# Moving a turn's second output addition, re-timing the steady table and merging the last two stores of a fused attention and feed-forward kernel

## The chip, the cores and the metric

The kernel runs on one core of a Trainium2 chip. The metric is the device time of one execution in microseconds (us). A program of one core is timed several times and the median is given. One more execution is taken with the hardware profiler, and every row below comes from that one.

## What is computed

The inputs are q, k and v of 8 batches, 8 heads, 576 tokens and 64 channels, phi of 32 memories for each token and head, and two weight matrices. The reference, cut to what matters:

```python
a = softmax(phi, axis=memories)
k_m, v_m = einsum("bhsm,bhsd->bhmd", a, k), einsum("bhsm,bhsd->bhmd", a, v)
attn = softmax(q @ k_m.T / sqrt(64)) @ v_m           # 32 memories per head
x = attn.transpose(0, 2, 1, 3).reshape(4608, 512)    # 8 batches of 576 tokens
h = x @ w_in                                         # 512 -> 2048
out = (h * clip(h + 3, 0, 6) / 6) @ w_out            # 2048 -> 512
```

All of it is float32. The kernel keeps that accuracy on TensorE by splitting each operand into a rounded high part and a low remainder, and by multiplying three times (high by high, high by low, low by high).

## The kernel before

v_m is never multiplied with the probabilities by itself. For each batch the kernel first folds v_m into w_in ("fold", line 457, in four chunks of 512 columns, names `fo.b.c`), so that the first product is probabilities times folded weights (`gemm1`, line 746, into the two PSUM tiles `ph`). The gated result goes into a second product with w_out (`products`, through `triple`, line 713). The folded weights come out of PSUM as a high part (`vh`, ScalarE, line 468) and a low part (`vl`, VectorE, line 477).

The first two batches run in an order that is written out word by word (`BEGIN`). The rest, from some 203 us on, is the steady part. A batch there is 32 **steps**; the tables `STEADY` and `EVERY` give each word of the attention work a step (`4 fo.C.3` means: in step 4, fold chunk 3 of the current batch C; N is the next batch, M the one after). A batch has two halves of 256 and 320 tokens, a half has eight **units**, and a unit takes two steps, one for each of its two 128-row pieces of the hidden layer:

- Step 2n: TensorE does `gemm1`, ScalarE `relu` (line 752), VectorE `gate` (line 765); ScalarE and VectorE split the first four blocks of the unit before into high and low (`high`, line 786, `low`, line 791, tiles of 512 columns).
- Step 2n+1: the same for the second piece, then the sums that the product scheme needs: `sum_first` on VectorE (line 775), `sum_second` on GpSimd (lines 779 and 780), and the split of three more blocks (384 columns).
- In both, the products of the unit of three steps before, and in every even step the loads of the w_out blocks ("streams", line 709) of the unit two ahead, three DMAs of 256 KB on SP's queue.

The scheme is one level of a seven-product block multiplication, so a half's result stands in four PSUM banks that have to be combined: this is the **turn**, in steps 1 to 4 and 17 to 20. `leave_first` and `leave_second` read the banks (ScalarE lines 819, 820, 825; VectorE lines 828, 829), `leave_third` does two additions on GpSimd (lines 833 and 834) and `store` writes the tile (line 839). The list `owed` holds what is still to be done: at the next odd step, behind that unit's sums, `leave_third` is called, and at the even step after it `store`.

The last 64 tokens of each batch ("rests") are collected for two batches and multiplied in a stage of their own at step 2 of every even batch and at the end (`rest_stage`). At an even batch the turn's additions and store, and the words of steps 0 to 2, are played inside that stage. At the very end `RestUnit.leave` reads two PSUM tiles of 256 columns with ScalarE (line 889) and stores each as two pieces of 64 rows, one for each batch (line 892): three pieces on SP's queue and the last on ScalarE's.

Loads run on SP's queue in the order of the program; a DMA that has to wait (for a buffer, for example) holds up those behind it. The w_in chunks lie in a ring of two tiles (`fetch.b.c.half`, line 213, 512 KB each), and five further buffers (`KV_RING`) are shared by the k and v tiles (line 234), the q tiles (line 244) and phi (line 228). The k and v tiles of a batch are last read by `mem.N` in step 11 (line 319, 80 matmuls).

Of the kernel before, what the change touches and what calls it, by code (L numbers as in the profile page):

```python
# [19 lines left out]
B, H, S, D, M = 8, 8, 576, 64, 32  # L20
# [6 lines left out]
REST = S - 4 * P  # L27
# [10 lines left out]
VC = 256  # L38
# [53 lines left out]
"""  # L92

STEADY = """
1 fo.C.3 vh.C.3.0 / 4 vl.C.3.0 / 8 vh.C.3.1 / 9 bh.C.1 vl.C.3.1 / 14 bl.C.1
"""

EVERY = """
2 sp.N / 7 xa.N.0 / 8 xe.N.0 xa.N.2 fetch.N.1.0 / 9 xe.N.2 xa.N.1 xe.N.1 / 10 fetch.N.0.0 / 11 mem.N / 12 q.N.1 nr.N
nk.N pt.M fetch.N.0.1 q.N.0 / 15 tp.N fetch.N.1.1 tk.N / 16 sb.N cp.N.2 / 17 cp.N.0 / 19 kv.M.0 cp.N.1 / 20 cm.N.0 /  # L100
21 fo.N.0 cm.N.1 / 22 cs.N.0 / 23 mx.M.0 vh.N.0.0 kv.M.1 vh.N.0.1 fetch.N.2.0 ex.N.0 vl.N.0.0 vl.N.0.1 ds.N.0
fetch.N.2.1 / 24 cs.N.1 mx.M.1 / 25 fo.N.1 vh.N.1.0 vl.N.1.0 dr.N.0 dm.N.0 / 26 fetch.N.3.0 vh.N.1.1 ex.N.1 pn.M
vl.N.1.1 mt.M bt.N.0 / 27 ds.N.1 kv.M.2 / 28 fo.N.2 vh.N.2.0 dr.N.1 dm.N.1 bh.N.0 kv.M.3 vl.N.2.0 / 29 kv.M.4 mo.M
fetch.N.3.1 bl.N.0 / 31 vh.N.2.1 bt.N.1 vl.N.2.1
"""

LATE = ()
# [3 lines left out]
def attention_ffn_kernel(ctx: ExitStack, tc: tile.TileContext, pn, pt, kv, kl, qt, w1, w2, out):  # L111
    nc = tc.nc
# [5 lines left out]
    sb = ctx.enter_context(tc.tile_pool(name="sb", bufs=1))  # L118
# [610 lines left out]
    class Unit:  # L729
# [101 lines left out]
        def leave_third(self):  # L831
            o, x = self.o, self.x
            nc.gpsimd.tensor_tensor(o[:, 1:3], x[:, 0:2], x[:, 2:4], ALU.add)
            nc.gpsimd.tensor_tensor(o[:, 0::3], o[:, 0::3], x[:, 1:3], ALU.add)

        def store(self):
# [7 lines left out]
    class RestUnit:  # L844
# [40 lines left out]
        def leave(self):  # L885
            if self.b == B - 2:
                for c in range(2):
                    o = sb.tile([P, VC], F32, name="o", **O_RING)
                    nc.scalar.mul(o, sums[self.b, 2][c], 1.0 / 6.0)
                    for k, queue in enumerate((nc.sync, nc.scalar if c else nc.sync)):  # L890
                        row = (self.b + k + 1) * S - REST
                        queue.dma_start(
                            out=out[row : row + REST, c * VC : (c + 1) * VC], in_=o[k * REST : (k + 1) * REST]
                        )
                return
            o = sb.tile([P, DM], F32, name="o", **O_RING)
            nc.scalar.mul(o[:, :VC], sums[self.b, 2][0], 1.0 / 6.0)
            nc.vector.tensor_scalar(o[:, VC:], sums[self.b, 2][1], 1.0 / 6.0, None, ALU.mult)
            for k in range(2):
                row = (self.b + k + 1) * S - REST  # L900
                nc.sync.dma_start(out=out[row : row + REST], in_=o[k * REST : (k + 1) * REST])
# [64 lines left out]
    with tc.manual_schedule():  # L966
# [32 lines left out]
        def half_step(i, between=None):  # L999
# [9 lines left out]
            unit, part = units[i // 2], i % 2  # L1009
# [8 lines left out]
            if unit.last:  # L1018
                (unit.leave_second if part else unit.leave_first)()
                if part and not between:  # L1020
                    owed[:] = unit.leave_third, unit.store
            return unit

        def finish_unit(unit, part):
# [13 lines left out]
        owed = []  # L1038
        total_steps = 2 * len(units)
        for s in range(total_steps + LAG + 1):  # L1040
# [8 lines left out]
            if s < total_steps:  # L1049
# [8 lines left out]
                if k:  # L1058
                    unit.sum_first()
                    unit.sum_second()  # L1060
                    if owed and len(owed) == 2:
                        owed.pop(0)()
                elif s >= 2 and not (resting and i == 2):
                    finish_unit(units[s // 2 - 1], 1)
# [8 lines left out]
                us[i].prepare()  # L1073
            unit = half_step(s - LAG - 1, (lambda: (us[3].total(), us[3].prepare())) if resting and i == 2 else None)
            if resting and i == 2:
                after = {2: [unit.leave_third, unit.store]} if unit else {}
                if b < B:
                    first = units[s // 2 - 1]
                    for k in range(3):
# [52 lines left out]
```

## Time and profile before

| | |
|---|---|
| median of 3 runs | 679.83 us (679.71 to 680.68) |
| the profiled execution's own time | 679.15 us |
| its span, first to last instruction | 677.3 us |
| TensorE matmul busy | 664.7 us, 98% of the span |
| VectorE / ScalarE / GpSimd busy | 567.9 / 397.0 / 350.8 us |
| DMA, mean over the span | 242 GB/s |

Matmuls overlap in the pipeline: one of 256 columns is listed with some 280 ns, while the next begins 113 ns after it. So the time between the starts of neighbouring matmuls tells what a matmul costs, and the busy share says little of how full the engine is. "Idle before" in a row is idle time of the engine ahead of it, with what ended it.

### The profile page before, as it was taken

The numbers are of one execution on the slowest core, as the hardware profiler recorded it, in microseconds if no ns is written. First come the engines' busy times: TensorE is split into PE (matmuls) and PEld (weight loads), VectorE is DVE, ScalarE is ACT, GpSimd is POOL, SyncE is SP. The second block draws the span as 40 slices with busy tenths as digits, with TensorE's granted clock in tenths as the row PEclk, the third lists the DMA queues.
The fourth block names the chain that finished last, engine by engine and source line by source line (L and its number), as shares of the span: only waits on it lengthen the run. The fifth ranks groups of instructions, "written<-read, shape, count | busy, mean of one in ns | idle before, by whom it ended". The sixth has DMA issues, their size and how long they took to land.

```text
span 677.3 us, 15517 instructions
## 1 busy us (share of the span) xinstructions
PE 664.7 (98%) x5890; PEld 579.3 (86%) x5894; DVE 567.9 (84%) x1070; ACT 397.0 (59%) x819; POOL 350.8 (52%) x356
## 2 busy tenths in 40 slices
PE   8999999999999999999999999999999999999997
PEld 3446787778779998899899998899989999899997
DVE  4899998988996779887997879977899779887865
ACT  4586787574654556655665655655565555655553
POOL 1644243898573337453654345554556246555533
PEclk9999999999999999999999999999999999999999
DMA  9998492355858968769591786949493594836351
GB/s 352 419 334 314 176 378 95 151 180 170 325 183 280 353 251 278 310 209 363 179 395 48 223 334 184 398 150 360 173 370 146 181 312 127 279 113 230 126 187 47
DMA packets 66820, 163.96 MB, mean 242 GB/s; under 512 B 7097, under 2 KB 12217, under 8 KB 64697
## 3 DMA queue, kind: packets, MB, share of 16 engines
q1 hardware_dynamic: 66664, 162.91, 67.4%
q8 instruction: 46, 0.75, 0.4%
q14 instruction: 30, 0.24, 0.1%
q10 hardware_dynamic: 80, 0.07, 0.0%
HBM read 140.92 MB, written 22.03 MB: 241 GB/s over the span
## 4 chain that ended last, share of the span: by engine, by line
PE 80%; DVE 12%; DMA 3%; ACT 3%; issue 1%; POOL 0%; SPq 0%; ACTq 0%; DVEq 0%
PE acc L713 35%; PE ph L746 18%; PE acc L574 10%; PE ph L520 7%; PE pv L457 4%; DVE rounded L791 3%; PE pk L319 2%; PE acc L911 2%; DMA w<-w_kept 2%; DVE gated L765 1%; DVE gated L775 1%; DVE both L477 1%; PE psc L387 1%; ACT rounded L786 1%; DVE gf L536 1%
## 5 line engine op out<-in xcount | busy, mean ns | idle before, releaser
L713 PE MATMUL acc<-w,rounded 128*128 128x256 f32 x1536 | 212.3, 280 | 1.6 <-DVE rounded L791 1.4
L713 PEld LDWEIGHTS acc<-w,rounded 128*128 128x128 f32 x1536 | 192.1, 188 | 21.9 <-ACT gf L752 11.7
L779 POOL TENSOR_TENSOR gated<-gated 128x256 f32<-128x256 f32 x96 | 92.9, 968 | 216.4 <-DVE gated L765 210.2
L791 DVE TENSOR_TENSOR rounded<-gated,rounded 128x384 fp32r<-128x384 f32 x192 | 158.0, 824 | 36.6 <-ACT rounded L786 35.9
L746 PE MATMUL ph<-probs,both 128*128 128x256 f32 (+1 forms) x1152 | 180.6, 292 | 0.0
L786 ACT CAST rounded<-gated 128x384 fp32r<-128x384 f32 x192 | 108.6, 567 | 112.7 <-DVE gated L775 103.4
L746 PEld LDWEIGHTS ph<-probs,both 128*128 128x128 f32 x1152 | 157.5, 188 | 1.0 <-issue 0.8
L752 ACT ACTIVATE gf<-ph,three 128x256 f32<-128x256 f32 (+1 forms) x192 | 95.9, 499 | 46.5 <-PE ph L746 45.4
L713 PE MATMUL acc<-stream,rounded 128*128 128x256 f32 x864 | 113.7, 276 | 0.0
L713 PEld LDWEIGHTS acc<-stream,rounded 128*128 128x128 f32 x864 | 105.2, 188 | 0.0
L765 DVE SCALAR_TENSOR_TENSOR gated<-gf,ph 128x256 f32<-128x256 f32 x192 | 79.0, 412 | 27.7 <-ACT gf L752 26.8
L574 PE MATMUL acc<-w,ghi 128*128 128x512 f32 x224 | 59.0, 396 | 0.0
L520 PEld LDWEIGHTS ph<-probs,both 128*128 128x128 f32 x336 | 47.1, 188 | 10.4 <-DVE gf L536 5.8
L520 PE MATMUL ph<-probs,both 128*128 128x320 f32 (+1 forms) x336 | 51.1, 299 | 1.4 <-DVE gf L536 0.9
L574 PEld LDWEIGHTS acc<-w,ghi 128*128 128x128 f32 x224 | 40.1, 188 | 10.9 <-ACT gf L530 1.7
L780 POOL TENSOR_TENSOR gated<-gated 128x128 f32<-128x128 f32 x96 | 49.1, 512 | 0.0
L775 DVE TENSOR_TENSOR gated<-gated 128x256 f32<-128x256 f32 x96 | 42.2, 439 | 1.6
L468 ACT CAST both<-pv 128x512 fp32r<-128x512 f32 x62 | 35.5, 585 | 13.5 <-PE pv L457 12.7
L477 DVE TENSOR_TENSOR both<-pv,both 128x512 fp32r<-128x512 f32 x62 | 41.1, 673 | 1.8 <-ACT both L468 1.5
L190 POOL TENSOR_TENSOR w<-tmp,raw 128x512 uint32<-128x512 uint32 x12 | 18.9, 1595 | 44.5 <-DVE tmp L180 27.1
L530 ACT ACTIVATE gf<-ph,three 128x576 f32<-128x576 f32 (+2 forms) x36 | 24.7, 690 | 23.2 <-PE ph L520 13.7
L457 PE MATMUL pv<-w,kvT 64*32 64x512 f32 (+1 forms) x528 | 35.1, 588 | 2.2 <-DMA w<-w_kept 0.9
(124 smaller groups left out, 862.5 us busy)
## 6 DMA issues: line engine op xcount, KB each, us to landing
stream<-kept SPq DMA_DIRECT2D x222, 256.0 KB, 4.5
w<-w_kept SPq DMA_DIRECT2D x40, 512.0 KB, 6.8
kvt<-in_kv SPq DMA_DIRECT2D x32, 516.0 KB, 6.2
raw<-in_w SPq DMA_DIRECT2D x16, 512.0 KB, 9.5
raw<-in_w SPq DMA_DIRECT2D x8, 1024.0 KB, 10.3
out_t<-o SPq DMA_DIRECT2D x16, 512.0 KB, 3.1
kept<-stage SPq DMA_DIRECT2D x24, 256.0 KB, 2.7
pnat<-in_pn SPq DMA_DIRECT2D x8, 576.0 KB, 7.9
```

Source lines behind the costliest of these rows:

```text
L457: nc.tensor.matmul(to[j * M : (j + 1) * M, g, k], self.kvT[rows, g, j * M : (j + 1) * M], chunk[rows, k, j].bitcast(F32), start=True, stop ...
L520: nc.tensor.matmul(dst, w[:, g, fs], x[:, g * n : (g + 1) * n], start=(i == 0), stop=(i == len(seq) - 1),)
L574: nc.tensor.matmul(accs[self.b, self.rest, k].rearrange("p (x c) -> p x c", c=VC), left[:, t * P : (t + 1) * P], w, start=k in self.first ...
L713: nc.tensor.matmul(dst, left[l], right[r], start=begin and n == 0, stop=end and n == 2, skip_group_check=True)
L746: nc.tensor.matmul(h, w[:, g, fs], x[:, g * self.n : (g + 1) * self.n], start=(i == 0), stop=(i == len(seq) - 1))
L752: nc.scalar.activation(self.gf, self.h[k], AF.Relu, bias=three)
L765: nc.vector.scalar_tensor_tensor(dst, by_tile(self.gf), 6.0, by_tile(self.h[k]), ALU.min, ALU.mult)
L775: nc.vector.tensor_tensor(g[:, 5:7], g[:, 7:9], g[:, 0:2], ALU.add)
L779: nc.gpsimd.tensor_tensor(g[:, 2:4], g[:, 0::8], g[:, 1:8:6], ALU.subtract)
L780: nc.gpsimd.tensor_tensor(g[:, 4], g[:, 1], g[:, 7], ALU.add)
L786: nc.scalar.copy(self.parts[0][:, at], self.g[:, 1:8][:, at])
L791: nc.vector.tensor_tensor(low[:, at], self.g[:, 1:8][:, at], high[:, at].bitcast(F32), ALU.subtract)
```

## The change

- `leave_third` is cut in two. Its second addition becomes `leave_fourth`, and `owed` now holds three calls. At a turn outside the rest stage the first addition stays behind the sums of the next odd step, the second comes behind those of the odd step after that, and the store two steps later than before. In the rest stage the order stays as it was.
- The steady tables are written anew. The fourth chunk's fold goes from step 1 to step 4 (with its `vh` and `vl`), one phi subtraction and exponential change places (`xa`, `xe`), q is loaded from step 9 instead of 12, the second half of chunk 0 returns at step 17 instead of 12, the k and v loads come earlier, the scores' transposes (`cp`) all in step 16.
- The last two stores: each tile of 128 rows is now written by one DMA, whose destination is seen as 2 batches by 64 rows by 256 columns; the first on SP's queue, the second on ScalarE's.

```diff
 STEADY = """
-1 fo.C.3 vh.C.3.0 / 4 vl.C.3.0 / 8 vh.C.3.1 / 9 bh.C.1 vl.C.3.1 / 14 bl.C.1
+4 fo.C.3 / 5 vh.C.3.0 vl.C.3.0 / 6 vh.C.3.1 / 8 bh.C.1 vl.C.3.1 / 14 bl.C.1
 """
 EVERY = """
-2 sp.N / 7 xa.N.0 / 8 xe.N.0 xa.N.2 fetch.N.1.0 / 9 xe.N.2 xa.N.1 xe.N.1 / 10 fetch.N.0.0 / 11 mem.N / 12 q.N.1 nr.N
-nk.N pt.M fetch.N.0.1 q.N.0 / 15 tp.N fetch.N.1.1 tk.N / 16 sb.N cp.N.2 / 17 cp.N.0 / 19 kv.M.0 cp.N.1 / 20 cm.N.0 /
...
+4 sp.N / 7 xa.N.0 / 8 fetch.N.0.0 xa.N.1 xe.N.0 fetch.N.1.0 / 9 q.N.1 xe.N.1 q.N.0 xa.N.2 / 10 xe.N.2 / 11 mem.N / 12
+nr.N nk.N / 14 pt.M / 15 tp.N tk.N / 16 cp.N.0 fetch.N.1.1 sb.N kv.M.0 cp.N.1 cp.N.2 / 17 fetch.N.0.1 / 20 cm.N.0 / 21
...
         def leave_third(self):
             o, x = self.o, self.x
             nc.gpsimd.tensor_tensor(o[:, 1:3], x[:, 0:2], x[:, 2:4], ALU.add)
+
+        def leave_fourth(self):
+            o, x = self.o, self.x
             nc.gpsimd.tensor_tensor(o[:, 0::3], o[:, 0::3], x[:, 1:3], ALU.add)
...
-                    for k, queue in enumerate((nc.sync, nc.scalar if c else nc.sync)):
-                        row = (self.b + k + 1) * S - REST
-                        queue.dma_start(
-                            out=out[row : row + REST, c * VC : (c + 1) * VC], in_=o[k * REST : (k + 1) * REST]
-                        )
+                    both = out[self.b * S :].rearrange("(k s) d -> k s d", k=2)[:, S - REST :]
+                    queue = nc.scalar if c else nc.sync
+                    queue.dma_start(
+                        out=both[:, :, c * VC : (c + 1) * VC], in_=o
+                    )
...
-                    owed[:] = unit.leave_third, unit.store
+                    owed[:] = unit.leave_third, unit.leave_fourth, unit.store
...
-                    if owed and len(owed) == 2:
+                    if len(owed) > 1:
                         owed.pop(0)()
...
-                after = {2: [unit.leave_third, unit.store]} if unit else {}
+                after = {2: [unit.leave_third, unit.leave_fourth, unit.store]} if unit else {}
```

**First place: VectorE, steps 3 to 6 of an odd batch, just behind the turn.** `both<-pv` is the low part of a folded chunk (`vl`), the other names are those of the section above. Before:

```order
L791 TENSOR_TENSOR rounded<-gated,rounded 128x512
L477 TENSOR_TENSOR both<-pv,both 128x512
L765 SCALAR_TENSOR_TENSOR gated<-gf,ph_2144 128x256
L775 TENSOR_TENSOR gated<-gated 128x256
L791 TENSOR_TENSOR rounded<-gated,rounded 128x384
```

and now:

```order
L791 TENSOR_TENSOR rounded<-gated,rounded 128x512
L765 SCALAR_TENSOR_TENSOR gated<-gf,ph_2144 128x256
L775 TENSOR_TENSOR gated<-gated 128x256
L477 TENSOR_TENSOR both<-pv,both 128x512
L791 TENSOR_TENSOR rounded<-gated,rounded 128x384
```

The low part of the folded chunk no longer stands ahead of step 5's gate, but behind its sum. On GpSimd the same stretch read before:

```order
L833 TENSOR_TENSOR o<-o 128x512
L834 TENSOR_TENSOR o<-o 128x2x256
L779 TENSOR_TENSOR gated<-gated 128x256
L780 TENSOR_TENSOR gated<-gated 128x128
L779 TENSOR_TENSOR gated<-gated 128x256
```

and now:

```order
L833 TENSOR_TENSOR o<-o 128x512
L779 TENSOR_TENSOR gated<-gated 128x256
L780 TENSOR_TENSOR gated<-gated 128x128
L837 TENSOR_TENSOR o<-o 128x2x256
L779 TENSOR_TENSOR gated<-gated 128x256
```

The second addition (834, now 837) stands behind the sums of step 5 instead of ahead of them.

**Second place: SP's queue, steps 10 to 14.** `kept_1_106` and its like are the three blocks of one unit's stream (here of the unit whose second part runs in step 14), `qh` the q tiles. Before:

```order
L213 DMA w_5029<-w_kept_81 128x1024
L709 DMA stream<-kept_1_106 128x512
L709 DMA stream<-kept_2_107 128x512
L709 DMA stream<-kept_0_105 128x512
L244 DMA qh<-in_qt 128x640 x2
L228 DMA ptile<-in_pt 128x576 x2
L213 DMA w_5029<-w_kept_81 128x1024
L244 DMA qh<-in_qt 128x1024
```

and now:

```order
L244 DMA qh<-in_qt 128x640 x2
L244 DMA qh<-in_qt 128x1024
L709 DMA stream<-kept_1_106 128x512
L709 DMA stream<-kept_2_107 128x512
L709 DMA stream<-kept_0_105 128x512
```

The q loads, whose buffers are those of the k and v tiles that step 11 reads, now stand ahead of step 10's stream.

**Third place: the end of ScalarE's queue.** Before:

```order
L865 CAST rounded<-total 128x128
L889 ACTIVATE o<-acc 128x256 x2
L892 DMA out_t<-o 64x256
L1128 UNCONDITIONAL_BRANCH
```

and now:

```order
L868 CAST rounded<-total 128x128
L892 ACTIVATE o<-acc 128x256 x2
L895 DMA out_t<-o 2x64x256
L1131 UNCONDITIONAL_BRANCH
```

The DMA's size is that of its destination: 64 rows of 256 before, 2 by 64 rows of 256 now. On SP's queue three such stores of 64 rows became one of 2 by 64.

## Rows read from the trace of the kernel before

**Rows 1.** Waits of PE: line waited for, us in total, times, longest.
```profile
PE acc L713 <- DVE rounded L791: 1.4, 4, 0.4
PE pv L457 <- DMA w<-w_kept: 0.9, 2, 0.6
```
**Rows 2.** PE's timeline at the fourth chunk's fold, batches 3 and 5: start us, us, what.
```profile
282.59 0.84 PE L746 MATMUL ph<-probs,both 128*128 128x256 f32 x6
283.69 1.09 PE L457 MATMUL pv<-w,kvT 64*32 64x512 f32 x16 [0.26 <-DMA w<-w_kept]
...
438.46 0.87 PE L746 MATMUL ph<-probs,both 128*128 128x256 f32 x6
439.97 1.09 PE L457 MATMUL pv<-w,kvT 64*32 64x512 f32 x16 [0.65 <-DMA w<-w_kept]
```
**Rows 3.** The same timeline at an undisturbed fold (step 21).
```profile
327.25 1.03 PE L746 MATMUL ph<-probs,both 128*128 128x320 f32 x6
328.22 1.09 PE L457 MATMUL pv<-w,kvT 64*32 64x512 f32 x16
```
**Rows 4.** PE's timeline at step 7 of batch 3, and step 23 of batch 7.
```profile
296.05 0.39 PE L713 MATMUL acc<-w,rounded 128*128 128x256 f32 x2
296.78 1.08 PE L713 MATMUL acc<-w,rounded 128*128 128x256 f32 x7 [0.34 <-DVE rounded L791]
...
639.93 1.56 PE L713 MATMUL acc<-w,rounded 128*128 128x256 f32 x9
```
**Rows 5.** The chain of waits from 290 to 297 us, its end.
```profile
292.48 1.37 DVE rounded L791
293.85 0.60 DVE both L477
...
295.87 0.86 DVE rounded L791
```
**Rows 6.** GpSimd's timeline in the same stretch.
```profile
291.69 1.61 POOL L833 TENSOR_TENSOR o<-o 128x512 f32<-128x512 f32 x1
293.26 1.74 POOL L834 TENSOR_TENSOR o<-o 128x512 f32<-128x512 f32 x1
```
**Rows 7.** VectorE's and PE's timeline at steps 6 to 9 of batch 3.
```profile
296.99 0.69 DVE L791 TENSOR_TENSOR rounded<-gated,rounded 128x512 fp32r<-128x512 f32 x1
...
299.54 0.81 DVE L791 TENSOR_TENSOR rounded<-gated,rounded 128x384 fp32r<-128x384 f32 x1
...
300.41 1.18 PE L713 MATMUL acc<-w,rounded 128*128 128x256 f32 x9
```
**Rows 8.** PE's timeline at steps 11 to 14 of batch 3.
```profile
306.52 1.30 PE L713 MATMUL acc<-w,rounded 128*128 128x256 f32 x9
...
312.43 0.84 PE L713 MATMUL acc<-stream,rounded 128*128 128x256 f32 x6
```
**Rows 9.** DMA issues from 303 to 313 us: KB each, median us to landing.
```profile
stream<-kept SPq DMA_DIRECT2D x7, 256.0 KB, 6.5
```
**Rows 10.** Timeline from 672.5 us: the last DMA issues of SP and ScalarE.
```profile
673.09 1.75 SPq L892 DMA_DIRECT2D out_t<-o  x3
...
673.78 0.56 ACTq L892 DMA_DIRECT2D out_t<-o  x1
```
**Rows 11.** DMA from 670 to 677.3 us: GB/s in 40 slices; packets by queue.
```profile
GB/s 0 0 0 0 0 0 0 0 0 0 0 0 0 0 0 0 0 0 0 0 0 0 0 151 185 23 50 208 219 208 191 185 17 0 0 0 0 0 0 0
...
q10 hardware_dynamic: 80, 0.07, 3.7%
...
out_t<-o ACTq DMA_DIRECT2D x1, 64.0 KB, 2.2
```
**Rows 12.** DMA from 70.8 to 73 us, around the store of the maxima.
```profile
DMA packets 48, 0.28 MB, mean 125 GB/s; under 512 B 13, under 2 KB 13, under 8 KB 16
...
nmx<-nmxT SPq DMA_DIRECT2D x1, 1.0 KB
```
**Rows 13.** DMA from 142.6 to 144.4 us, stores of 1 KB rows: GB/s, 40 slices.
```profile
GB/s 91 205 296 364 341 364 319 364 364 319 296 364 341 319 387 364 341 342 342 364 319 319 364 341 319 364 387 341 364 319 341 341 341 319 524 228 524 159 592 364
```

More of the change, by code (lines that the diff above doesn't have):

```diff
@@ L94 @@
 STEADY = """
-1 fo.C.3 vh.C.3.0 / 4 vl.C.3.0 / 8 vh.C.3.1 / 9 bh.C.1 vl.C.3.1 / 14 bl.C.1
+4 fo.C.3 / 5 vh.C.3.0 vl.C.3.0 / 6 vh.C.3.1 / 8 bh.C.1 vl.C.3.1 / 14 bl.C.1
 """
 EVERY = """
-2 sp.N / 7 xa.N.0 / 8 xe.N.0 xa.N.2 fetch.N.1.0 / 9 xe.N.2 xa.N.1 xe.N.1 / 10 fetch.N.0.0 / 11 mem.N / 12 q.N.1 nr.N
-nk.N pt.M fetch.N.0.1 q.N.0 / 15 tp.N fetch.N.1.1 tk.N / 16 sb.N cp.N.2 / 17 cp.N.0 / 19 kv.M.0 cp.N.1 / 20 cm.N.0 /
[L101 to L104, printed above, removed]
+4 sp.N / 7 xa.N.0 / 8 fetch.N.0.0 xa.N.1 xe.N.0 fetch.N.1.0 / 9 q.N.1 xe.N.1 q.N.0 xa.N.2 / 10 xe.N.2 / 11 mem.N / 12
+nr.N nk.N / 14 pt.M / 15 tp.N tk.N / 16 cp.N.0 fetch.N.1.1 sb.N kv.M.0 cp.N.1 cp.N.2 / 17 fetch.N.0.1 / 20 cm.N.0 / 21
+cm.N.1 fo.N.0 / 22 cs.N.0 kv.M.1 / 23 mx.M.0 vh.N.0.0 kv.M.4 kv.M.2 cs.N.1 vh.N.0.1 fetch.N.2.0 ex.N.0 vl.N.0.0
+vl.N.0.1 ds.N.0 fetch.N.2.1 / 24 mx.M.1 / 25 fo.N.1 vh.N.1.0 vl.N.1.0 fetch.N.3.0 dr.N.0 dm.N.0 / 26 vh.N.1.1 ex.N.1
+vl.N.1.1 mt.M bt.N.0 pn.M / 27 ds.N.1 dr.N.1 mo.M / 28 fo.N.2 fetch.N.3.1 dm.N.1 vh.N.2.0 bh.N.0 kv.M.3 / 29 vl.N.2.0
+/ 30 vh.N.2.1 bl.N.0 / 31 vl.N.2.1 bt.N.1
 """
```

## The prediction

> **What bounds the kernel now.** I read the page first: TensorE is busy for 98% of the span, so only two kinds of time can go: time in which TensorE waits, and what follows its last matmul. The waits of PE say how little the first is: 1.4 us behind VectorE's low part (line 791) in 4 places, 0.9 us behind the return of a w_in chunk in 2 [rows 1]. Everything else that this change moves lies beside matmuls. These waits are counted from a modelled end, so I size them again from starts in PE's timeline; for what leads up to them I read the chain of waits there, GpSimd's timeline beside it, and the DMA view for the loads and the last stores.
>
> **What the fold's move gives.** At an undisturbed fold, six matmuls of 320 columns start at 327.25 and the fold at 328.22, 0.97 later [rows 3]; at 0.147 a matmul that is 0.88 and 0.09 for the switch. Six of 256 columns at 0.113 make 0.68 + 0.09 = 0.77. In batch 3 the fold came 283.69 - 282.59 = 1.10 after its predecessors, 0.33 late; in batch 5 439.97 - 438.46 = 1.51, 0.74 late [rows 2]. Both wait for the second half of chunk 3. In step 4 instead of 1, with that load issued a step earlier, the fold has some four steps or 8 us to spare where it was short of 0.74, so both waits go: **-1.07 us**. The fold's own 1.09 [rows 3] moves whole, and costs the same in step 4 as in step 1.
>
> **What the turn gives.** In step 7 of batch 3 two products start at 296.05; the third should start 0.23 later, at 296.28, and starts at 296.78: 0.50 lost, and 0.11 more, since the seven that follow take 1.08 [rows 4] where 6 x 0.113 + 0.28 = 0.97 is usual. Two more such places, in step 7 of batches 5 and 7, measure the same (the 4 of [rows 1]), and step 23 of batch 7 loses 0.38: nine matmuls take 1.56 [rows 4] where 1.18 is usual [rows 7]. Together 3 x 0.61 + 0.38 = 2.21 us. The chain there runs through VectorE alone: the 512-column low part takes 1.37, then the folded chunk's low part 0.60, then the gate [rows 5]. The 512-column part takes 0.69 elsewhere [rows 7]; here GpSimd's two additions, 1.61 and 1.74 long, run beside it [rows 6]. The change takes both out of the way: the folded chunk's part goes behind the gate and the sum, where VectorE waited for ScalarE anyway, and the second addition goes behind the next sums. Step 4's fold gives VectorE another 1 us ahead of step 5. **-2.21 us.**
>
> **What is late next.** The second addition now runs beside the 512-column low part of step 6, which can take 1.37 for 0.69 there: up to 0.7 later. The low part of step 7 ended at 299.54 + 0.81 = 300.35, and the products that need it began at 300.41 [rows 7]: 0.06 to spare in the old order. From the new order I count about 0.1 of reserve, so some of it will come back. It costs nothing at best and 0.7 at worst, in batches 3 and 5 (batch 7 has no phi work there); I take 0.2 each, since the fold's 1 us stands ahead: **+0.4**. The rest of the tables I cost at nothing. The transposes of step 16 fall into a stretch in which VectorE waited for ScalarE; the later phi remainder must be through ScalarE before the last of the 80 memory matmuls, which I count to be met by 0.1 to 0.5; chunk 0's second half returns in step 17 for a fold in step 21, four steps or 8 us for a load that [rows 9] let take 6 to 7. The store two steps later frees a buffer that is wanted 12 steps on.
>
> **What the last stores cost.** This term decides. Now four stores of 64 rows leave at 673.09 (three on SP, 1.75 together) and 673.78 (ScalarE) [rows 10]; bytes flow from 674.2 (slice 24) to 676.0 (slice 33) [rows 11]. Merging spares SP two issues. But how many DMA engines carry a store follows its shape. A store of 64 rows counts 80 packets, 64 rows and 16 closing ones, one for each engine [rows 11]. The store of the maxima, 4 by 2 pieces, stands in a stretch with 13 small packets [rows 12]: 8 pieces leave at most 5 closing ones, where 16 engines would have made 24 packets. So a destination that begins with 4 went over 4 engines, and one that begins with 2, as the merged stores', should go over 2. All other large transfers here begin with 64 rows or more. With 2 engines each store puts 64 rows of 1 KB on one engine, and if both stores use the same two, 128 rows. The price of a row has two rows to bound it: stores of 1 KB rows from all 128 partitions run at 341 to 364 GB/s [rows 13], over 16 engines 45 to 48 ns a row; the old last stores, from 64 partitions, at some 208 [rows 11], 79 ns. The merged store reads 128 partitions, so I take 47: 128 x 0.047 = 6.0 us, the last bytes at 674.2 + 6.0 = 680.2 instead of 676.0, **+4.2 us** (4.0 at 45 ns, 8.3 at 79 ns). Nothing covers it: TensorE has ended.
>
> On this the Trainium skill, "DMA: Bandwidth & Descriptors", section "Why a DMA increments its semaphore by 16 and not by 1", says that the engines are the largest number up to 16 that divides the slowest dimension of both sides, here 2 and 128. By that rule it is 2 engines; the 13 packets agree for a destination of 4, and no run here shows one of 2. The same page's "Rules for kernel authors" advises one transfer of 128 partitions in place of two of disjoint halves, which taken alone would make the merge a small gain; that is rival B.
>
> **The sum.** -1.07 - 2.21 + 0.4 + 4.2 = +1.3 us on the profiled execution's 679.15: 680.45. That execution lies 0.68 below the median, so the median becomes **681.1 us**, from 679.83. A difference under 0.2% (1.36 us, so 678.5 to 681.2) is about what a measurement of this kernel can't tell from none: the forecast is no change, at its upper edge.
>
> **Case A, the forecast (0.59).** Gain 1.8 to 3.3, end 4.0 to 5.0: 680.5 to 683.0.
>
> **Rival B, all 16 engines take part in the merged stores (0.20).** Then SP's third issue, which ends 0.5 after ScalarE's (674.84 against 674.34) [rows 10], is spared and four more rows an engine take 0.2 to 0.3 of it back: -0.2 and no +4.2. With -2.9 from the steady part, 679.83 - 3.1 = 676.7. For it: the stores of 64 rows went over 16, and the merged ones' source has 128 rows [rows 11]. Against: the maxima's store [rows 12].
>
> **Rival C, the stream of step 14 comes late (0.13).** q's loads now stand on SP ahead of step 10's stream, and they wait for the k and v tiles, the last of which is free when the 80 matmuls end at 306.5 [rows 8]. The three streams then leave at some 307.1 instead of 302.99, and are wanted at 312.43 [rows 8], 5.3 later. Streams in this stretch took 6.5 from issue to landing [rows 9], though behind 1.1 MB that now follows them, while 1.2 MB of q stand ahead. It decides at 5.3. At 6.5 it costs 1.2 in each of the five batches with a next one, 6.0 in all; half of that on A gives 684.1. On top of B it would eat the gain.
>
> **Rival D, a row costs 79 ns on two engines as well (0.08).** End +8.3: 679.83 - 2.9 + 8.3 = 685.2.
>
> **The numbers.** The range reaches from just under B to just over A: 676.4 to 683.6, which leaves out most of C and D. Faster by over 0.2% comes from B and a sliver of A: 0.21. A puts over half of its 0.59 within the 0.2%, with a sliver of B 0.35. The rest of A, C and D are slower: 0.44.
>
> **What the changed profile would show.** The waits of PE behind the w_in chunk and in step 7 gone, and the last matmul some 2.9 us earlier. In step 9 of batches 3 and 5 a wait of 0 to 0.7 behind line 791. In the last microseconds two of 16 engines, a DMA share of an eighth and 40 to 45 GB/s for 6 us, some 260 packets instead of 320, and SP waiting about 6 us for the last store. Were that stretch as short as now, B is right; a wait of line 713 behind a stream in step 14 would be C; a rate of some 26 GB/s at the end, D.

## The result, and the profile after

The changed kernel takes **689.8 us** (median of 4 runs, 689.52 to 691.24), the kernel before beside it 679.77 (679.57 to 680.68): a ratio of 1.0149, 95% interval 1.0132 to 1.0167, some 10 us slower. 681.1 was forecast, and the range ended at 683.6; rival C at its full 6.0 on top of the forecast would have been 687.1. The profiled execution took 689.68 us over a span of 687.9, against 679.15 and 677.3: 10.5 more.

**The turns and the fold.** The waits of PE after 195 us, the steady part of the changed kernel (line waited for, us in total, times, longest):

```profile
PE acc L713 <- DMA stream<-kept: 1.5, 3, 1.0
PE acc L713 <- DVE rounded L791: 0.4, 1, 0.4
```

Both waits of [rows 1] are gone from the turns and the fold. The one that is left behind line 791 stands at 666.14, behind the last step; the kernel before has it too, at 660.01, as one of the 4 of [rows 1]. So only three of those 4 were the turn's, each in step 7. PE's timeline there, step 7 of batch 3 and, between, the fold in step 4 (start us, us, what):

```profile
290.23 0.84 PE L746 MATMUL ph<-probs,both 128*128 128x256 f32 x6
291.01 1.09 PE L457 MATMUL pv<-w,kvT 64*32 64x512 f32 x16
...
297.25 0.84 PE L746 MATMUL ph<-probs,both 128*128 128x256 f32 x6
297.93 1.18 PE L713 MATMUL acc<-w,rounded 128*128 128x256 f32 x9
```

The fold starts 0.78 after its predecessors instead of 1.10 [rows 2], and nine products of step 7 take 1.18 in one piece where they were torn in two [rows 4]. Measured from start to start of the steps, step 7 of batches 3, 5 and 7 gained 0.62, 0.63 and 0.63, step 23 of batch 7 0.37, the fold's move some 0.8 over the batches: 3.05 in all.

**The end.** ScalarE's and SP's last issues, and SP's wait for the last store:

```profile
678.81 0.38 ACT L892 ACTIVATE o<-acc 128x256 f32<-128x256 f32 x1 [2.79 <-PE acc L713]
679.22 0.57 SPq L895 DMA_DIRECT2D out_t<-o  x1
679.49 0.38 ACT L892 ACTIVATE o<-acc 128x256 f32<-128x256 f32 x1 [0.30 <-PE acc L713]
679.91 1.12 ACTq L895 DMA_DIRECT2D out_t<-o  x1
```

```profile
SPq L1131 <- DMA out_t<-o: 7.0, 1, 7.0
```

And the DMA view from 678 to 687.9 us, in 40 slices of 0.25 us:

```profile
DMA  0000000000111111111111111111111111000000
GB/s 0 0 0 0 0 0 0 0 0 12 29 33 37 21 37 46 17 33 50 50 50 50 46 46 50 50 50 50 46 46 50 50 50 50 17 0 0 0 0 0
DMA packets 260, 0.26 MB, mean 26 GB/s; under 512 B 4, under 2 KB 260, under 8 KB 260
...
q10 hardware_dynamic: 130, 0.13, 3.7%
```

Each store is 130 packets, 128 rows and 2 closing ones (together the 4 under 512 B), where a store of 64 rows had 16 closing ones [rows 11]. With 260 packets, a busy share of one to two tenths and 46 to 50 GB/s I read this as two of the 16 engines; a row of 1 KB then takes one of them 41 to 45 ns. From ScalarE's last read to the end of the span it is 687.9 - 679.49 = 8.4 us; before, that read began at 673.36, and it was 677.3 - 673.36 = 3.9. The end costs **4.5** (+4.2 was forecast).

**What is left.** The last read itself should have come 2.9 earlier and came 679.49 - 673.36 = 6.1 us **later**. So the steady part lost some 9 us that the prediction did not have. A third of it is in one place, step 14 of the five batches that have a next one. SP's issues and PE's timeline in batch 3:

```profile
300.50 1.87 SPq L709 DMA_DIRECT2D stream<-kept  x3
306.37 1.28 SPq L244 DMA_DIRECT2D qh<-in_qt  x3
307.70 4.20 SPq L709 DMA_DIRECT2D stream<-kept  x6
```

SP's wait for the last k and v matmuls (line 319) with the q loads, in the whole run:

```profile
SPq L244 <- PE pk L319: 18.7, 5, 4.3
```

```profile
313.50 0.50 PE L713 MATMUL acc<-w,rounded 128*128 128x256 f32 x3
313.84 1.79 PE L713 MATMUL acc<-stream,rounded 128*128 128x256 f32 x9
```

q stands ahead of step 10's streams and waits for the last k and v matmuls until 306.37 (five such waits of up to 4.3 us; before, none was over 0.9), so the streams leave from 307.70 on, where they left at 302.99. They then stop TensorE three times by some 0.2: nine products take 1.79 where 1.18 is usual. None of these stops is long enough to be listed in brackets; the waits of PE show 1.5 us behind streams in the whole steady part, step 14 alone loses 0.62, 0.61, 0.61, 0.93 and 0.57, 3.3 in all, and step 12 of batch 5 1.0. The other place is the seam between two batches, steps 28 to 0 (batch 5 here), together 3.9:

```profile
436.66 0.84 PE L713 MATMUL acc<-stream,rounded 128*128 128x256 f32 x6
438.49 0.62 PE L713 MATMUL acc<-stream,rounded 128*128 128x256 f32 x3 [0.98 <-DMA stream<-kept]
```

There the DMA engines have no room. The windows view gives their share as the last but one column (us from start to end; then busy us of PE, PEld, DVE, ACT and POOL, granted clock, DMA share, GB/s); two stretches of the changed kernel, and then the nearest ones of the kernel before:

```profile
281.00:284.00 3.00, 2.61 (x20) 2.21 (x20) 3.00 (x8) 1.79 (x4) 1.33 (x2) 1.00 1.01 375
434.00:440.00 6.00, 5.02 (x40) 4.82 (x39) 5.43 (x11) 3.34 (x7) 3.85 (x4) 1.00 1.04 406
```

```profile
277.50:281.00 3.50, 3.50 (x31) 3.50 (x30) 3.09 (x7) 2.43 (x5) 2.47 (x4) 1.00 1.05 404
432.50:438.50 6.00, 6.00 (x52) 6.00 (x51) 5.42 (x12) 3.85 (x8) 4.55 (x6) 1.00 1.03 404
```

The engines were full there before, too. What differs is when the streams leave. The chain of waits ahead of 438.49, and SP's three streams of step 26, now and before:

```profile
423.22 7.19 DMA w<-w_kept
430.50 7.94 DMA stream<-kept
```

```profile
427.71 3.11 SPq L709 DMA_DIRECT2D stream<-kept  x3
```

```profile
424.47 1.91 SPq L709 DMA_DIRECT2D stream<-kept  x3
```

The stream that stops TensorE is the last of these three. Step 26 starts at 425.96 now and started at 422.73 before, so the three have left 4.9 us after the step's start, where it was 3.7. By the chain SP issues the last one when the return of a w_in chunk has landed; it then takes 7.9 to land itself. The same stream leaves later against its step at all four seams, by 0.6 to 2.5 us.

### The profile page after: what moved, and what is told of

It reads as the page before. It is cut to its first block, busy times and chain, and to the rows that moved or that the text cites. A ratio compares the mean times of both kernels' runs of the same rounds, so it can differ in the third digit from the quotient of the medians.

```text
span 687.9 us, 15489 instructions
## 1 busy us (share of the span) xinstructions
PE 670.8 (98%) x5890; PEld 581.9 (85%) x5894; DVE 578.5 (84%) x1070; ACT 398.1 (58%) x819; POOL 348.6 (51%) x356
## 4 chain that ended last, share of the span: by engine, by line
PE 81%; DVE 7%; DMA 7%; ACT 2%; issue 1%; POOL 0%; SPq 0%; ACTq 0%; DVEq 0%
PE acc L713 37%; PE ph L746 19%; PE acc L574 10%; PE ph L520 6%; PE pv L457 4%; DMA stream<-kept 3%; DMA w<-w_kept 3%; PE acc L914 2%; PE pk L319 2%; DVE rounded L791 1%; PE psc L387 1%; DVE gf L536 1%; DMA raw<-in_w 1%; DVE glo L554 0%; DVE gated L765 0%
## 5 line engine op out<-in xcount | busy, mean ns | idle before, releaser
L791 DVE TENSOR_TENSOR rounded<-gated,rounded 128x384 fp32r<-128x384 f32 x192 | 164.4, 857 | 28.6 <-ACT rounded L786 27.7
L713 PE MATMUL acc<-stream,rounded 128*128 128x256 f32 x864 | 119.5, 280 | 1.8 <-DMA stream<-kept 1.5
L713 PEld LDWEIGHTS acc<-stream,rounded 128*128 128x128 f32 x864 | 106.9, 188 | 6.1 <-DMA stream<-kept 5.8
L780 POOL TENSOR_TENSOR gated<-gated 128x128 f32<-128x128 f32 x96 | 46.9, 489 | 0.0
```

The costliest lines, as they stand in the source:

```text
L713: nc.tensor.matmul(dst, left[l], right[r], start=begin and n == 0, stop=end and n == 2, skip_group_check=True)
L780: nc.gpsimd.tensor_tensor(g[:, 4], g[:, 1], g[:, 7], ALU.add)
L791: nc.vector.tensor_tensor(low[:, at], self.g[:, 1:8][:, at], high[:, at].bitcast(F32), ALU.subtract)
```

## The experiments

Every kernel was timed in 5 rounds beside the kernel before on its chip. "Against before" is the ratio less one, times the median of the kernel before there, with its 95% interval. The chips differ, and so the kernels are compared through that column. The times of one kernel spread over 2 to 6 us here, more than its interval, and one execution of each was profiled: the shortest one of a1, a3 and c1, the longest of b2, c3 and e2. So losses added up over the steps of a profile need not meet the medians.

| run | what it is | us | against before |
|---|---|---|---|
| a1_old_stores | changed, four old last stores | 684.98 | +4.9 (3.2 to 6.6) |
| a2_stores_only | before, merged last stores | 684.90 | +4.9 (3.8 to 5.9) |
| e2_one_merged | before, one of the two merged | 682.06 | +1.8 (0.8 to 2.7) |
| a3_addition_only | before, later addition and store | 683.41 | +3.1 (2.0 to 4.2) |
| a4_fold_only | before, new row for the fourth chunk | 678.42 | -1.4 (-2.1 to -0.6) |
| d1_store_late | a4 with a later store, addition as before | 679.53 | -1.2 (-2.2 to -0.2) |
| b3_order | a4 with the later addition and store | 680.04 | -0.1 (-1.0 to +0.8) |
| g1_fold_again | a4 once more | 678.67 | -1.6 (-2.4 to -0.7) |
| g2_addition_on_fold | b3 once more, beside g1 | 679.11 | -1.3 (-2.2 to -0.3) |
| b4_every_only | before, new table `EVERY` | 687.74 | +8.0 (7.1 to 8.9) |
| b1_q_back | a1, q in step 12 | 680.58 | +0.4 (-0.3 to +1.1) |
| h1_q_early | a4, q in step 9 | 681.63 | +1.6 (0.7 to 2.5) |
| b2_kv_back | a1, k and v as before | 687.78 | +8.2 (6.7 to 9.6) |
| c1_addition_back | a1, addition and store as before | 684.57 | +4.4 (3.0 to 5.6) |
| c4_q_addition_back | b1, addition and store as before | 680.06 | -0.5 (-1.4 to +0.3) |
| c3_q_kv_addition_back | c4, k and v as before | 681.06 | +1.0 (0.0 to 1.8) |
| f1_weights_back | c4, returns of weights as before | 678.90 | -1.4 (-2.2 to -0.5) |
| h2_addition_weights_back | b1, returns of weights as before | 678.59 | -2.0 (-2.9 to -1.1) |

### The last stores

a1 puts the old stores into the changed kernel, a2 the new ones into the kernel before:

```diff
-                    both = out[self.b * S :].rearrange("(k s) d -> k s d", k=2)[:, S - REST :]
-                    queue = nc.scalar if c else nc.sync
-                    queue.dma_start(
-                        out=both[:, :, c * VC : (c + 1) * VC], in_=o
-                    )
+                    for k, queue in enumerate((nc.sync, nc.scalar if c else nc.sync)):
+                        row = (self.b + k + 1) * S - REST
+                        queue.dma_start(
+                            out=out[row : row + REST, c * VC : (c + 1) * VC], in_=o[k * REST : (k + 1) * REST]
+                        )
```

> The changed kernel with the four old stores of 64 rows at its end; all else as changed. Theory 1 (the merged stores go over two DMA engines, and that alone lengthens the end by the 4.46 us that lie between the two profiles): 689.8 - 4.5 = 685.3 us. Rival (the end is longer for another reason, so that the form of the stores costs nothing): 689.8 us. Rival (the merge itself saves SP an issue that is now paid again): 0.5 more than theory 1, 685.8 us. In the profile theory 1 wants last bytes some 3 us after the last read of the sums, as in the kernel before.

> The kernel before with the merged last stores alone. Theory 1: 679.8 + 4.5 = 684.3 us, and the steady part as before, TensorE's last matmul within 0.1 us of 672.8. Rival (no cost of the merge): 679.8 us or a few tenths less.

a1 comes to 684.98 and a2 to 684.90: taking the merge away gives 10.1 - 4.9 = 5.2 us, putting it in costs 4.9 (3.8 to 5.9). e2 merges only the first pair, in the kernel before:

```diff
+                    if c == 0:
+                        both = out[self.b * S :].rearrange("(k s) d -> k s d", k=2)[:, S - REST :]
+                        nc.sync.dma_start(out=both[:, :, :VC], in_=o)
+                        continue
                     for k, queue in enumerate((nc.sync, nc.scalar if c else nc.sync)):
```

> The kernel before with the first of the two last pairs of stores merged, the second pair as it was. Theory 1 (rows over two engines set the end, 43 ns each): 64 rows an engine make 2.8 us and start 0.3 to 0.5 before the last store's rows would; with 8 rows of the old pair, 679.8 + 1.5 to 2.2 = 681.3 to 682.0 us. Rival 1 (the end is a fixed cost of a store with two outer pieces, not of its rows): 684.5 us. Rival 2 (the first store is hidden behind the second pair): 679.8 us.

It costs 1.8 (0.8 to 2.7). SP's last wait and its DMA view in e2 (between 7.0 with both merged and 1.4 with none):

```profile
SPq L1132 <- DMA out_t<-o: 3.8, 1, 3.8
```

```profile
q1 hardware_dynamic: 251, 0.25, 10.7%
q10 hardware_dynamic: 80, 0.07, 2.0%
...
out_t<-o SPq DMA_DIRECT2D x1, 64.0 KB, 4.3
out_t<-o ACTq DMA_DIRECT2D x1, 64.0 KB, 4.5
```

ScalarE's plain store has 80 packets again; SP's queue has 130 for the merged store, 80 for the plain one, and 41 of a store before. The plain ones land 4.3 and 4.5 after their issue where it was 2.2 [rows 11], behind the merged one's rows. Half the merge costs about a third of the whole, between the 4.9 of a fixed cost and the nothing of a hidden one, and within the 1.5 to 2.2 worked out from the rows on two engines: the cost follows the rows, not the form of the store as such.

### The fold, the later addition and the turn

a4 is one line of the table, a3 the division of `leave_third`, each in the kernel before:

```diff
-1 fo.C.3 vh.C.3.0 / 4 vl.C.3.0 / 8 vh.C.3.1 / 9 bh.C.1 vl.C.3.1 / 14 bl.C.1
+4 fo.C.3 / 5 vh.C.3.0 vl.C.3.0 / 6 vh.C.3.1 / 8 bh.C.1 vl.C.3.1 / 14 bl.C.1
```

```diff
+        def leave_fourth(self):
+            o, x = self.o, self.x
             nc.gpsimd.tensor_tensor(o[:, 0::3], o[:, 0::3], x[:, 1:3], ALU.add)
...
-                    owed[:] = unit.leave_third, unit.store
+                    owed[:] = unit.leave_third, unit.leave_fourth, unit.store
```

> The kernel before with the second output addition (and with it the store) a unit later; both tables and the last stores as before. Theory 1 (the addition beside VectorE's 512-column low part is what makes step 7 late): the four waits go, 679.8 - 2.2 = 677.6 us. Rival 1 (the folded chunk's low part ahead of the gate is what makes it late; the addition is harmless): 679.8 us. Rival 2 (the store, two steps later and ahead of the loads of weights, is what makes the streams late at the ends of the batches, 3.7 us by the step table): 677.6 + 3.7 = 681.3 us.

> The kernel before with the new row for the fourth chunk's fold alone: fold in step 4, its parts behind the gate in step 5 and on. Theory 1 (the fold gives 0.8 in sum over the batches, the turn is cured by the addition): 679.8 - 0.8 = 679.0 us. Rival 1 (the folded chunk's low part behind the gate cures the turn as well): 679.8 - 0.8 - 2.2 = 676.8 us. Rival 2 (neither can be had alone; VectorE gets the fold's parts and the addition together in step 5): 680.0 us or more.

The later addition by itself makes the kernel **slower**, by 3.1 us. Its waits of PE after 195 us, PE's timeline in steps 7 and 9 of batch 3, and VectorE's and GpSimd's there:

```profile
PE acc L713 <- DVE rounded L791: 1.9, 6, 0.4
```

```profile
297.31 1.08 PE L713 MATMUL acc<-w,rounded 128*128 128x256 f32 x7 [0.28 <-DVE rounded L791]
...
301.68 1.09 PE L713 MATMUL acc<-w,rounded 128*128 128x256 f32 x7 [0.35 <-DVE rounded L791]
```

```profile
293.00 1.43 DVE L791 TENSOR_TENSOR rounded<-gated,rounded 128x512 fp32r<-128x512 f32 x1
294.35 0.68 DVE L477 TENSOR_TENSOR both<-pv,both 128x512 fp32r<-128x512 f32 x1
...
297.52 1.43 DVE L791 TENSOR_TENSOR rounded<-gated,rounded 128x512 fp32r<-128x512 f32 x1
```

```profile
292.27 1.61 POOL L833 TENSOR_TENSOR o<-o 128x512 f32<-128x512 f32 x1
...
296.80 1.60 POOL L837 TENSOR_TENSOR o<-o 128x512 f32<-128x512 f32 x1
```

One addition beside it is enough to stretch VectorE's 512-column low part to 1.43. With two additions a unit apart, two low parts are slow, step 7 is as late as before, and step 9 is late as well. Step 9 of batches 3, 5 and 7 loses 0.65, 0.63 and 0.20 there, half of the 3.1; the rest is streams at the seams.

The fold's row by itself does most for the turn. VectorE's and PE's timeline in a4:

```profile
292.64 1.44 DVE L791 TENSOR_TENSOR rounded<-gated,rounded 128x512 fp32r<-128x512 f32 x1
294.00 0.41 DVE L765 SCALAR_TENSOR_TENSOR gated<-gf,ph 128x256 f32<-128x256 f32 x1
294.44 1.07 DVE L775 TENSOR_TENSOR gated<-gated 128x256 f32<-128x256 f32 x1
295.44 0.68 DVE L477 TENSOR_TENSOR both<-pv,both 128x512 fp32r<-128x512 f32 x1
296.10 0.86 DVE L791 TENSOR_TENSOR rounded<-gated,rounded 128x384 fp32r<-128x384 f32 x1
```

```profile
296.79 1.32 PE L713 MATMUL acc<-w,rounded 128*128 128x256 f32 x9
```

The 512-column part is as slow as ever; but the folded chunk's part (line 477) is no longer ahead of the gate, and step 7 gains 0.49, 0.44 and 0.45 of its 0.62. The second addition now only slows the sum (1.07 for 0.42 elsewhere). In the changed kernel, with both edits, step 7 gains the rest. Step 9 loses 0.16 and 0.17 in batches 3 and 5 there, but 0.11 and 0.16 in a4 as well, where no addition runs beside step 6's low part. Step 9's products in batch 3, in a4 and in the changed kernel (1.18 before):

```profile
300.69 1.30 PE L713 MATMUL acc<-w,rounded 128*128 128x256 f32 x9
```

```profile
301.67 1.34 PE L713 MATMUL acc<-w,rounded 128*128 128x256 f32 x9
```

So this loss comes with the fold's row, and the later addition adds next to nothing to it, although it does stretch step 6's low part to 1.44 in the changed kernel.

What the later addition is worth on top of the fold took three more kernels: b3 is a4 with it; d1 moves the store alone.

```diff
-                    owed[:] = unit.leave_third, unit.store
+                    owed[:] = unit.leave_third, lambda: None, unit.store
```

> The kernel before with the new row for the fourth chunk and the later second addition, the old table of loads and the old last stores. Theory 1 (the later store costs some 2.3 us in the streams at the ends of the batches, as in the run with the addition alone; step 9's 0.65 in two batches is gone, since the fold is out of the way): 678.4 - 0.9 for the rest of step 7 and step 23 of batch 7 + 2.3 = 679.8 us. Rival 1 (with the fold moved, the later addition is free): 678.4 - 0.9 = 677.5 us. Rival 2 (its cost of 3.6 us adds in full): 682.0 us.

> The kernel before with the new row for the fourth chunk, both additions where they were, and the store alone issued a unit later. Theory 1 (the later place of 0.5 MB in the queue makes streams late at the batches' ends): 678.4 + 2.3 = 680.7 us. Rival (the cost of the later addition is VectorE's low part beside it, in step 9, and the store itself is free): 678.4 us.

> The kernel before with the new row for the fourth chunk alone, now on the same chip as the three beside it. Theory: 1.4 us below the kernel before, as first measured. It is the base that the next three are read against.

> The same with the later second addition and store, beside it on one chip. Theory 1 (the later addition gains 0.9 in the turns' rest and loses 2.3 in streams at the batches' ends): 1.4 us above the fold alone. Rival 1 (the difference between the two chips' runs made it): 0.8 us below the fold alone. Rival 2 (gain and loss cancel): level with it.

b3 came out 1.3 above the fold alone (-0.1 against -1.4), on different chips; on one chip, g2 is 0.3 above g1. The two intervals overlap: on the fold the later addition gives back at least what it gains in the turns (by the steps 0.13 + 0.19 + 0.18 in step 7 and 0.37 in step 23 of batch 7, 0.87 in sum), and costs between 0.3 and 1.3 on top. Where it loses that is open. The later store alone does not cost the 2.3 of theory 1: d1 is level with the fold (-1.2), where that theory had +0.9. A smaller part is not excluded: behind streams in step 2 of an even batch, where a4 loses nothing, the profiles lose 0.8 in b3 (batch 4) and 0.6 and 0.4 in d1 (batches 4 and 6).

### q ahead of the streams

b1 is a1 with q's words back in step 12 (here and below the table is written a step a line):

```diff
-9 q.N.1 xe.N.1 q.N.0 xa.N.2
+9 xe.N.1 xa.N.2
...
-12 nr.N nk.N
+12 q.N.1 q.N.0 nr.N nk.N
```

> The changed kernel with the four old last stores, and the two q loads issued in step 12 again, behind step 10's streams. Against the same without that (685.0 us): theory 1 (the streams of step 14 are late because q stands ahead of them on SP; step 14 lost 2.4 in sum there) says 685.0 - 2.4 = 682.6 us, or 681.8 where step 12 of batch 5 gains its 0.8 too. Rival (the streams of step 14 are late because the transfers are slow, wherever they stand): 685.0 us.

680.58, or 4.5 below a1 (+0.4 against +4.9). SP's issues and step 14 of batch 3:

```profile
300.30 4.96 SPq L709 DMA_DIRECT2D stream<-kept  x6
305.95 1.36 SPq L244 DMA_DIRECT2D qh<-in_qt  x3
```

```profile
313.42 1.18 PE L713 MATMUL acc<-stream,rounded 128*128 128x256 f32 x9
```

q leaves at 305.95, nearly when it left in the changed kernel (306.37), since it waits for the same matmuls; only the streams have changed their place. Step 14 loses 0.00 in all five batches, and step 12 of batch 5 nothing either. In the changed kernel's profile these two make 3.3 + 1.0 = 4.4, in a1's 2.4 + 0.8 = 3.2 (that execution took 682.1 us, below a1's median).

> The kernel before with the new table of the next batch's steps alone; fold, addition and last stores as before. Theory 1 (the table alone brings the late streams of step 14, of step 12 in batch 5 and of the batches' ends): 679.8 + 2.4 + 0.8 + 2.6 = 685.6 us. Rival 1 (the ends' share comes from the later store): 679.8 + 3.2 = 683.0 us. Rival 2 (the table costs nothing by itself): 679.8 us.

The table `EVERY` by itself (the kernel before with it) costs 8.0; on top of the fold's row it costs 5.8 (c1's +4.4 against -1.4). Step 14 loses 1.5, 0.8, 0.9, 0.7 and 0.9 there.

h1 puts q into step 9 of a4, and of the other loads only the first half of chunk 0 a step earlier, so that it stays ahead of q:

```diff
-8 xe.N.0 xa.N.2 fetch.N.1.0
-9 xe.N.2 xa.N.1 xe.N.1
-10 fetch.N.0.0
...
-12 q.N.1 nr.N nk.N pt.M fetch.N.0.1 q.N.0
+8 xe.N.0 xa.N.2 fetch.N.1.0
+9 fetch.N.0.0 q.N.1 xe.N.2 q.N.0 xa.N.1 xe.N.1
...
+12 nr.N nk.N pt.M fetch.N.0.1
```

> The kernel before with the new row for the fourth chunk, and of the table of loads one thing: q's two loads in step 9, ahead of step 10's streams on SP (the first half of chunk 0 a step earlier, so that it stays ahead of them). Theory 1 (q ahead of the streams is enough by itself): the fold alone + 4.4, that is 2.7 to 3.0 us above the kernel before, with a later step 14 in all five batches. Rival 1 (it costs only together with the k, v and weight loads of the changed table): level with the fold alone, 1.4 below the kernel before. Rival 2 (half and half): 0.8 us above.

1.6 above the kernel before, 3.0 above the fold alone: q's place is enough for two thirds of its cost, and step 14 loses 2.7 in h1's profile (0.90, 0.05, 0.47, 0.82, 0.47), with nothing late at the seams. SP's issues in h1:

```profile
304.87 1.39 SPq L244 DMA_DIRECT2D qh<-in_qt  x3
306.32 2.15 SPq L709 DMA_DIRECT2D stream<-kept  x3
```

### k, v and the returns of weights

The seams remain. The theory was that 0.77 MB of k and v, pulled into step 23, fill the queue ahead of the streams. b2 puts them back in a1:

```diff
-16 cp.N.0 fetch.N.1.1 sb.N kv.M.0 cp.N.1 cp.N.2
+16 cp.N.0 fetch.N.1.1 sb.N cp.N.1 cp.N.2
+19 kv.M.0
...
-22 cs.N.0 kv.M.1
-23 mx.M.0 vh.N.0.0 kv.M.4 kv.M.2 cs.N.1
+23 mx.M.0 vh.N.0.0 kv.M.1 cs.N.1
...
+27 ds.N.1 kv.M.2 dr.N.1 mo.M
...
+29 kv.M.4 vl.N.2.0
```

> The changed kernel with the four old last stores, and the five k and v loads issued in steps 19, 23, 27, 28 and 29 as before. Theory 1 (0.77 MB of k and v pulled into step 23 put every later stream behind a full queue; the ends and starts of the batches lost 2.6 in sum) says 685.0 - 2.6 = 682.4 us. Rival 1 (the store, now in step 22 and ahead of the same streams, does it; the kv loads are hidden): 685.0 us. Rival 2 (both share it): about 683.7 us.

The theory fell: +8.2 instead of +4.9. The waits of PE in b2:

```profile
PE acc L713 <- DMA stream<-kept: 4.9, 8, 1.5
```

By the steps of that profile, b2's longest execution, steps 14 and 15 lose 8.3 where a1 lost 2.4, and the seams into batches 3 to 6 lose 6.0 where a1 lost 2.6. So the earlier k and v loads help; how late ones delay step 14 with q ahead of the streams was not followed up. The weights' returns were asked next, with and without the others:

```diff
-8 fetch.N.0.0 xa.N.1 xe.N.0 fetch.N.1.0
+8 xa.N.1 xe.N.0 fetch.N.1.0
...
-10 xe.N.2
+10 fetch.N.0.0 xe.N.2
...
-12 q.N.1 q.N.0 nr.N nk.N
+12 q.N.1 nr.N nk.N fetch.N.0.1 q.N.0
...
-17 fetch.N.0.1
...
-28 fo.N.2 fetch.N.3.1 dm.N.1 vh.N.2.0 bh.N.0 kv.M.3
+28 fo.N.2 dm.N.1 vh.N.2.0 bh.N.0 kv.M.3
+29 fetch.N.3.1 vl.N.2.0
```

(and `fetch.N.1.1` from step 16 to 15; `fetch.N.3.0` stays where the change has it). c1, c4 and c3 put back the addition, the addition and q, and all three with k and v.

> The changed kernel with the four old last stores, and the second addition and the store where they were, a unit earlier; q and all other loads as changed. Theory 1 (the later store costs the same 1.6 here as on top of the fold's move): 685.0 - 1.6 = 683.4 us. Rival 1 (the new table has made room for it, so only the turn's rest comes back): 685.0 + 0.9 = 685.9 us. Rival 2 (store and q compete for the same place in the queue, so without the late store q costs less): under 682.5 us.

> The changed kernel with the four old last stores, q in step 12 again, and the second addition and the store a unit earlier; k, v and weights as changed. Theory 1 (what is left of the loss, 1.6 to 2, is the later store's): 680.6 - 1.6 = 679.0 us, and the streams at the batches' starts in time. Rival (it is the other loads', now earlier or later than before): 680.6 us, or 681.4 with the turn's rest come back.

> The changed kernel with the four old last stores, q in step 12, the second addition a unit earlier, and k and v in steps 19 to 29 as before; weights and vector work as changed. Theory 1 (late k and v loads cost in this table even with q back): 2 us above the run with k and v as changed, 1.5 us above the kernel before. Rival (they cost only with q early): 0.5 to 1.4 us below the kernel before.

> The changed kernel with the four old last stores, q in step 12, the second addition a unit earlier, and the returns of the weights in the steps of before; k, v and all vector work as changed. With the run that has the weights as changed (0.5 below the kernel before) it tells the weights' part, with the fold alone (1.4 below) the part of k and v. Theory 1 (the earlier k and v loads help the batches' ends, as the run with them put back had it): 2 to 4 us below the kernel before. Rival 1 (k and v matter only where q stands early): 1.4 us below. Rival 2 (the k and v loads are what is left of the loss): 0.5 us below.

> The changed kernel with the four old last stores, q in step 12 and the returns of weights as before: what is left of the change is the fold, the later second addition, the earlier k and v and the order of the vector work. Theory (the earlier k and v make room for the later store, so that the addition's 0.8 in the turns is kept): 2.2 us below the kernel before. Rival (the store costs what the turns give, as on the fold alone): 1.3 us below. Rival (it costs more here): level with the kernel before.

With the weights as changed, q back and the old addition: +1.0 with late k and v, -0.5 with early ones. The late kind (its longest execution was profiled) loses 1.08, 1.42, 1.01 and 1.75 in step 0 of batches 3 to 6. Its waits behind streams:

```profile
PE acc L713 <- DMA stream<-kept: 2.1, 4, 0.8
```

With the weights as before it is -1.4 to -1.6 either way (f1 with early k and v, the fold alone with late ones). So the weights' new places cost 0.9 with early k and v, a difference that the intervals do not clear. With late ones it is 2.4 to 2.6, but there the order of the vector work differs as well, since the fold alone has the old one; earlier k and v seem to make up for part of it. With the weights and q back, and the later addition kept, h2 comes to **-2.0 (-2.9 to -1.1)**, the fastest of all, though its interval overlaps the fold's. Against b1 (+0.4, -0.3 to +1.1), which differs in these returns alone, that is 2.4, clear of both intervals; and by the steps the seams lose 3.7 in b1's profile and 1.2 in h2's. c1 is level with a1 (+4.4 to +4.9), so there no effect of the addition's place is seen.

Along one chain of single edits, from the changed kernel to the kernel before: last stores 5.2 (10.1 to 4.9), q 4.5 (4.9 to 0.4), the weights' returns 2.4 (0.4 to -2.0; 0.9 in the pair without the later addition), and the rest, fold, addition, k and v and the vector work's order, a gain of 2.0. Each difference has an uncertainty of 1 to 2 us. Which of the four returns does it was not tried.

## Why the prediction was wrong

- **The end: right.** +4.2 was forecast, 4.5 lies between the profiles, 4.9 and 5.2 between the times. The 47 ns a row were 41 to 45, and the first rows came slower. The Trainium skill, "DMA: Bandwidth & Descriptors", section "Why a DMA increments its semaphore by 16 and not by 1", gave two engines for a slowest dimension of 2; the 130 packets agree. The same page of the Trainium skill, section "Rules for kernel authors", advises one transfer of 128 partitions in place of two halves, and here that cost 4.9: the destination's shape decides. Rivals B and D are out.
- **The fold: right**, -0.8 for -1.07. Both waits behind the chunk went.
- **The turn: the size right, the cause half wrong.** -2.21 was forecast and 2.25 measured. But "the change takes both out of the way" is not what happens: the first addition alone keeps the 512-column part at 1.43 (a3, a4, and the changed kernel). The count of waits was also misread: one of the 4 in [rows 1] is not at a turn and stayed; the sum does not rest on it. Some 1.4 of the 2.25 come from the folded chunk's part going behind the gate, 0.9 from the later addition. The prediction named both and did not divide.
- **The give-back: the size right by luck, the cause wrong.** 0.16 and 0.17 were measured in step 9 for 0.2 each. But step 9 loses 0.11 and 0.16 with the fold's row alone (a4), without the later addition that I had blamed. The low part beside that addition is slow as forecast (1.44), and with the fold moved it costs next to nothing. Without the fold's move (a3) it costs 0.65, near the 0.7 that I had as the bound.
- **The step that failed: "The rest of the tables I cost at nothing."** It has two parts. Rival C was the case, and I gave it 0.13. Its mechanism stands as written: q ahead of the streams, these leaving at 307.70 (307.1 was worked out), too late for step 14; its price was 3.0 to 6.0, and 4.5 was measured (b1), 3.0 with q moved in a4 (h1). That 4.5 lies in the middle is in part luck: C priced step 14 alone, which lost 3.3 by the profile, and 1.0 more went in step 12 of batch 5. The numbers for it were in the text: 5.3 us to spare against 6.5 from issue to landing, with 1.2 MB of q ahead of them in place of 1.1 MB of other loads; I let a doubt about the queue weigh more than a row that said 1.2 us late. The other part had no rival at all: chunk 0's return and the store were costed by their own due time ("four steps or 8 us for a load that [rows 9] let take 6 to 7"), the other returns and the k and v loads not at all. No matmul of the steady part waits for any of these; what they push back was not asked. The streams at the seam, behind engines that were already full (1.03 to 1.05), are what came late: 3.9 by the steps, 2.4 by the run that undoes the weights. Which move makes up the rest of the 3.9 stays open.
- **The sum.** Gains, give-back and end together were -0.8 - 2.25 + 0.3 + 4.5 = +1.8 by the profile, for +1.3 forecast. The other 8.7 are 4.4 behind q, 3.9 at the seams, and 0.4 in smaller bits.

## What to carry to other kernels

Where the DMA engines are full, a moved load is not priced by its own due time alone, but also by what then stands behind it on its queue: for each moved issue, list the transfers that it now precedes, when they leave and when they are wanted. A load that waits for a buffer goes behind those that don't, since the queue stands still with it (here until 306.37, with the streams behind q leaving from 307.70). When two stores are merged, look at the outermost dimension of both sides first, and count the packets: the closing ones tell how many engines took part.

## What the runs showed of the hardware that was not expected

- One addition on GpSimd of 1.6 us is enough to stretch a VectorE operation with two tiles from SBUF from 0.69 to 1.43 us; a second one in its wake adds nothing to it, but slows the next such operation (1.07 for 0.42). The gate, which reads one of its tiles from PSUM, stayed at 0.41. The Trainium skill, "GPSIMD Engine Reference", section "1. Specifications", names contention with VectorE instructions in a 2-port mode or with two SBUF inputs; these rows agree with the second.
- Late transfers of a tenth or two each are nearly invisible among the waits: 1.5 us are listed behind streams in the steady part of the changed kernel, where steps 12 and 14 and the seams lost 8.3. The lengths of equal groups (nine products in 1.79 or 1.18) show them.
- The times of a1 lie between 682.1 and 687.9, those of the kernel before in the same rounds between 678.8 and 682.4. That transfers which come just in time make the wider spread is a guess; no run tests it.
